# Float64 weight conversion in an attention and two-layer expert kernel: upper words scaled by 2^-112 on ScalarE, clamp pass on VectorE left out

## The chip, the cores and the metric

The kernel runs on one core of one Trainium2 chip. The metric is the device time of one execution in microseconds. Five engines work side by side: TensorE (PE in the rows, its weight loads PEld), VectorE (DVE), ScalarE (ACT), GpSimd (POOL) and the DMA queues, most of which SyncE (SP) issues. Each engine works through its own instructions in the order of the program.

## The reference

The reference is a sliding-window attention (4 batches, 8 heads, 576 positions, head size 64, window 64) and, on its 2304 x 512 output, two gated layers one after the other:

```python
x = attention(q, k, v)                               # 2304 x 512
g = x @ moe_w_gate
x = (g / (1 + exp(-g)) * (x @ moe_w_val)) @ moe_w_out
g = 1 / (1 + exp(-(x @ moe2_w_gate)))
out = (g * (x @ moe2_w_val)) @ moe2_w_out
```

q, k and v are float32. [...]

## The kernel before, in words

Each weight matrix is cut into 12 blocks of 128 x 512 numbers; with six matrices that makes 72 conversions. One conversion goes like this. SyncE loads the block as pairs of words into a tile `raw` (`load_raw`, L374); there are four such tiles, so the load for a later block waits until the conversion four blocks earlier has read its tile for the last time. `round_a` then puts two instructions on ScalarE: L392 reads the lower words as unsigned integers, scales them by 2^-29 and writes integers, which gives the rounded lowest bits; L395 copies the upper words, read as if they were float32, into a tile `t` with the sign taken off (`Abs`). `round_b` puts four on VectorE: L403 picks the sign bit out of a 16-bit quarter of each number and sets the top exponent bit beside it; L404 clamps `t` between 2^-15 and 122816; L405 shifts `t` left by 3 bits; L406 adds the words that L392 and L403 wrote. The result is the weight in float32. L404 reads what L395 wrote, L405 reads what L404 wrote, and L406 reads what L405 wrote.

All products run in a split form: a float32 operand is cut into an upper part that ScalarE copies (`split_hi` L430 for weights, `x_hi` L343 for attention output, L970 for the hidden values) and the rest, which VectorE subtracts (`split_lo` L434, `x_lo` L346, L888). Three products of parts make one product.

The program is written out as a hand-made schedule. It has these stages:

- The start: the attention of the first four blocks of 128 tokens, with the first six conversions between them, in the order of the list `START` (`ca` is `round_a`, `cb` is `round_b`, `hi` and `lo` are L343 and L346, `ch` and `cl` the weight splits).
- The first layer, in five tiles of 512 or 384 tokens. Each tile has 12 rounds of three groups of 12 matmuls on TensorE: gate product (L448), value product (L448), output product (L459). Beside each group a table of due steps (`before`, `during`, `after`, filled by `at`) adds other work to the queues: the attention of the next tile's blocks and conversions. All remaining 30 conversions of the first layer's weights lie in the first of these tiles, which ends near 165 us in the profile; the second layer's 36 lie in the tiles after it, until 531 us.
- The second layer (L781, L846), which works on weights that are already converted.

The attention of one block takes these steps: transposes into PSUM (L205), copies out of it on ScalarE (`qt` L214, `kt` L220), scores (L247), masking on VectorE (L266), exponentials on ScalarE (L284, with an activation table load of its own), normalizing (L305 on ScalarE in the first tile, L309 on VectorE elsewhere), transposes (L317), copies (L323) and the product with v (L333). ScalarE also does the gate function (L961, which has a table load of its own) and stores each split output weight to DRAM (`store_parts`, L417). From the first tile to the end of the second, SyncE also rearranges q and k of later blocks through DRAM in many small pieces (`to_squares`, L136).

Of the kernel before, what the change touches and what calls it, by code (L numbers as in the profile page):

```python
# [8 lines left out]
FP32 = mybir.dt.float32  # L9
# [4 lines left out]
ACTF = mybir.ActivationFunctionType  # L14
ALU = mybir.AluOpType
# [1 line left out]
DRAM = bass.MemoryType.DRAM  # L17


F64_LEAST = 2.0 ** -15  # L20
F64_MOST = 122816.0

# [15 lines left out]
def attention_moe_moe(  # L40
# [20 lines left out]
    nc = tc.nc  # L61
# [7 lines left out]
    scale = 1.0 / float(D) ** 0.5  # L69
# [307 lines left out]
    def words_of(r):  # L377
        w = r.rearrange("p (f two) -> p f two", two=2)
        half = r.bitcast(UINT16).rearrange("p (f four) -> p f four", four=4)
        return w[:, :, 0], w[:, :, 1], half[:, :, 1], half[:, :, 3]  # L380
# [6 lines left out]
    def round_a(key):  # L387
        t = t_p.tile([128, 512], INT32, tag="t", name="t")
        mids[key] = t
        if wide:  # L390
            lower, upper, _, _ = words_of(raws[key])
            nc.scalar.activation(  # L392
                out=lower, in_=lower.bitcast(UINT32), func=ACTF.Copy, scale=2.0 ** -29
            )
            nc.scalar.activation(out=t.bitcast(FP32), in_=upper.bitcast(FP32), func=ACTF.Abs)  # L395

    def round_b(key):
        r = raws.pop(key)
        t = mids[key]
        tf = t.bitcast(FP32)  # L400
        if wide:
            lower, _, second, fourth = words_of(r)
            nc.vector.tensor_scalar(second, fourth, 0x8000, 0x4000, ALU.bitwise_and, ALU.bitwise_or)  # L403
            nc.vector.tensor_scalar(tf, tf, F64_LEAST, F64_MOST, ALU.max, ALU.min)  # L404
            nc.vector.tensor_scalar(t, t, 3, None, ALU.logical_shift_left)  # L405
            nc.vector.tensor_tensor(out=t, in0=t, in1=lower, op=ALU.add)  # L406
        else:
            nc.vector.tensor_copy(tf, r)
        mids[key] = tf
# [150 lines left out]
    def conv_b(j):  # L560
        round_b(convs[j][1])
        raw_ahead(j + 1 + 4)

    for j, (s, key) in enumerate(convs[SPLIT_EARLY:], SPLIT_EARLY):
        at(during, s + 1, round_a, key)
        at(during, s + 2, round_b, key)
        at(during, s + 2, raw_ahead, j + 1 + 4)
        plan_split(s + 2, key)
        if key[1] == "o":
            at(during, s + 5, store_parts, key)  # L570
# [20 lines left out]
    def operands(u, j, nm, following):  # L591
# [34 lines left out]
        def away(k):  # L626
# [3 lines left out]
            nc.sync.dma_start(out=wd[j, k][:, "gv".index(nm)], in_=stages[k][0].bitcast(FP32))  # L630

        at(during, u - 4, round_a, keys[0])
        at(during, u - 3, round_b, keys[0])
        at(during, u - 1, sums, 0)
        at(during, u - 1, upper, 0)
        at(during, u - 1, round_a, keys[1])
        at(during, u, lower, 0)
        at(during, u, round_b, keys[1])
# [253 lines left out]
    with tc.manual_schedule():  # L892
# [4 lines left out]
        t = ps_m.tile([128, 512], FP32, tag="a3", name="warm")  # L897
# [141 lines left out]
```

## Time and profile before

| what | value |
|---|---|
| time, median of 3 runs | 975.62 us |
| lowest and highest run | 974.51 and 978.52 us |
| profiled execution, span from first to last instruction | 977.2 us |
| mean granted TensorE clock in it | 0.985 of full speed |
| busy: TensorE, VectorE, ScalarE | 949.6, 646.1, 464.8 us |

The page gives no other time for the profiled execution than its span, so the span stands for it here. Busy time of TensorE counts a matmul from its start to its modelled end, and matmuls overlap, so a busy share near 100% doesn't say that every slot is used. A line such as L448 is a line of the kernel above; "<-ACT z L305" behind an idle time names the instruction that ended it.

### The profile page before, as it was taken

The numbers are of one execution on the slowest core, as the hardware profiler recorded it, in microseconds if no ns is written. First come the engines' busy times: TensorE is split into PE (matmuls) and PEld (weight loads), VectorE is DVE, ScalarE is ACT, GpSimd is POOL, SyncE is SP. The second block draws the span as 40 slices with busy tenths as digits, with TensorE's granted clock in tenths as the row PEclk, the third lists the DMA queues.
The fourth block names the chain that finished last, engine by engine and source line by source line (L and its number), as shares of the span: only waits on it lengthen the run. The fifth ranks groups of instructions, "written<-read, shape, count | busy, mean of one in ns | idle before, by whom it ended". The sixth has DMA issues, their size and how long they took to land.

```text
span 977.2 us, 15819 instructions
## 1 busy us (share of the span) xinstructions
PE 949.6 (97%) x5693; PEld 846.6 (87%) x5693; DVE 646.1 (66%) x1473; ACT 464.8 (48%) x1042; POOL 19.8 (2%) x39
## 2 busy tenths in 40 slices
PE   8799999999999999999999999999999999999998
PEld 6677777898878887888899999998899988999986
DVE  6999995656765666656566566688366695566742
ACT  6797985765555555356344331245212253222332
POOL 2101010000000000000000000000000000000000
PEclk7899999999999999999999999999999999999999
DMA  9677796999967664874689757634876625867411
GB/s 223 193 217 238 234 261 166 306 248 233 302 222 223 196 206 136 287 241 147 223 288 382 246 184 253 236 114 130 278 267 227 224 81 198 286 236 251 141 33 64
DMA packets 191774, 210.63 MB, mean 216 GB/s; under 512 B 93136, under 2 KB 135632, under 8 KB 191696
## 3 DMA queue, kind: packets, MB, share of 16 engines
q1 hardware_dynamic: 185360, 199.27, 64.5%
q10 hardware_dynamic: 5376, 7.21, 2.0%
q0 software_dynamic: 960, 3.15, 1.1%
q8 instruction: 45, 0.74, 0.3%
q14 instruction: 33, 0.27, 0.1%
HBM read 168.69 MB, written 46.40 MB: 220 GB/s over the span
## 4 chain that ended last, share of the span: by engine, by line
PE 80%; ACT 9%; DVE 6%; DMA 2%; issue 1%; SPq 0%; ACTq 0%; DVEq 0%
PE a L781 13%; PE g L448 12%; PE a L459 11%; PE v L448 11%; PE att L781 7%; PE a L846 7%; PE att L846 3%; PE v L781 3%; PE g L781 3%; ACT z L284 3%; PE g L846 3%; PE v L846 3%; PE att L333 1%; PE att L247 1%; DMA raw<-in_moe_w_out_dram 1%
## 5 line engine op out<-in xcount | busy, mean ns | idle before, releaser
L448 PE MATMUL g<-x,wg 128*128 128x512 f32 (+1 forms) x720 | 161.9, 374 | 0.8 <-ACT x L343 0.7
L448 PE MATMUL v<-x,wv 128*128 128x512 f32 (+1 forms) x720 | 161.9, 373 | 0.0
L459 PE MATMUL a<-h,wo 128*128 128x512 f32 (+1 forms) x720 | 161.2, 372 | 0.0
L448 PEld LDWEIGHTS g<-x,wg 128*128 128x128 f32 x720 | 133.0, 191 | 19.3 <-ACT x L343 0.8
L448 PEld LDWEIGHTS v<-x,wv 128*128 128x128 f32 x720 | 131.1, 190 | 16.8
L459 PEld LDWEIGHTS a<-h,wo 128*128 128x128 f32 x720 | 129.5, 188 | 18.5 <-issue 1.9
L781 PE MATMUL a<-xs,wop 128*128 128x384 f32 x756 | 136.2, 334 | 0.0
L781 PEld LDWEIGHTS a<-xs,wop 128*128 128x128 f32 x756 | 131.5, 188 | 0.1
L968 DVE TENSOR_TENSOR s<-s,v 128x512 f32<-128x512 f32 (+1 forms) x60 | 38.0, 633 | 104.1 <-PE v L448 74.1
L773 ACT ACTIVATE s<-s 128x384 f32<-128x384 f32 x72 | 37.9, 526 | 82.2 <-DVE s L767 82.2
L781 PE MATMUL att<-xs,wop 128*128 128x384 f32 x384 | 71.7, 334 | 0.0
L846 PE MATMUL a<-wo,hs 128*128 128x512 f32 x288 | 71.2, 389 | 0.0
L970 ACT ACTIVATE h<-s 128x512 fp32r<-128x512 f32 (+1 forms) x60 | 35.1, 585 | 75.4 <-DVE s L968 75.4
L961 ACT ACTIVATE s<-g 128x512 f32<-128x512 f32 (+1 forms) x60 | 33.2, 554 | 76.3 <-PE g L448 75.8
L781 PEld LDWEIGHTS att<-xs,wop 128*128 128x128 f32 x384 | 67.1, 188 | 0.1
L846 PEld LDWEIGHTS a<-wo,hs 128*128 128x128 f32 x288 | 54.0, 188 | 11.1
L403 DVE TENSOR_SCALAR raw<-raw 128x512 uint16<-128x512 uint16 x72 | 54.3, 755 | 6.5 <-ACT raw L392 6.3
L284 ACT ACTIVATE z<-z,nm 128x128 f32<-128x128 f32 x144 | 55.8, 390 | 3.2 <-DVE nm L266 3.0
L392 ACT ACTIVATE raw<-raw 128x512 int32<-128x512 uint32 x72 | 48.2, 669 | 9.6 <-DMA raw<-in_moe_w_out_dram 8.9
L406 DVE CUSTOM_DVE_ANT_0 t<-raw,t 128x1024 uint16<-128x1024 uint16 x72 | 50.1, 696 | 2.5
L767 DVE TENSOR_TENSOR s<-s,a 128x384 f32<-128x384 f32 x65 | 35.1, 553 | 22.9 <-PE a L781 22.6
L430 ACT ACTIVATE wo<-tw 128x512 fp32r<-128x512 f32 x36 | 22.6, 627 | 54.1 <-PE a L846 26.0
(131 smaller groups left out, 1323.3 us busy)
## 6 DMA issues: line engine op xcount, KB each, us to landing
wop<-wd SPq DMA_DIRECT2D x126, 512.0 KB, 5.9
wo<-k0o SPq DMA_DIRECT2D x48, 512.0 KB, 5.0
wd<-stage SPq DMA_DIRECT2D x36, 512.0 KB, 5.1
raw<-in_moe_w_gate_dram SPq DMA_DIRECT2D x24, 512.0 KB, 5.4
raw<-in_moe_w_val_dram SPq DMA_DIRECT2D x24, 512.0 KB, 5.5
raw<-in_moe_w_out_dram SPq DMA_DIRECT2D x24, 512.0 KB, 5.0
tw<-k1o SPq DMA_DIRECT2D x36, 256.0 KB, 3.0
k0o<-wo ACTq DMA_DIRECT2D x12, 512.0 KB, 5.1
```

Of the source, the lines that this page charges most:

```text
L284: nc.scalar.activation(out=z[:, hp, :], in_=z[:, hp, :], func=ACTF.Exp, scale=-1.0, bias=nm[:, hp:hp + 1], accum_out=su[:, hp:hp + 1],)
L392: nc.scalar.activation(out=lower, in_=lower.bitcast(UINT32), func=ACTF.Copy, scale=2.0 ** -29)
L403: nc.vector.tensor_scalar(second, fourth, 0x8000, 0x4000, ALU.bitwise_and, ALU.bitwise_or)
L406: nc.vector.tensor_tensor(out=t, in0=t, in1=lower, op=ALU.add)
L448: nc.tensor.matmul(out=ps[:, 0:n], lhsT=w[:, a, c, :], rhs=xt[:, b, c, 0:n], start=(j == 0), stop=(j == len(mm) - 1),)
L459: nc.tensor.matmul(out=acc[e][:, 0:n], lhsT=w[:, a, e * 128:(e + 1) * 128], rhs=h[:, b, 0:n], start=(fc == 0 and j == 0), stop=(fc == FC - ...
L767: nc.vector.tensor_tensor(out=to[out], in0=to[a], in1=ps, op=ALU.add)
L773: nc.scalar.activation(out=to[which], in_=to[which], func=ACTF.Sigmoid)
L781: nc.tensor.matmul(out=ps, lhsT=w[:, val, a, c, :], rhs=xops[op, b][:, c], start=(n == 0), stop=(n == len(mm) - 1),)
L846: nc.tensor.matmul(out=acc[e], lhsT=h[e // 3][:, a, e % 3 * 128:(e % 3 + 1) * 128], rhs=w[:, b], start=(fc == 0 and n == 0), stop=(fc == F ...
L968: nc.vector.tensor_tensor(out=s, in0=s, in1=vps[:, 0:n], op=ALU.mult)
L970: nc.scalar.activation(out=h[:, 0, 0:n], in_=s, func=ACTF.Copy)
```

## The change

The upper words are no longer read with the sign taken off. ScalarE copies them with a scale of 2^-112 (the same kind of instruction with another function and another scale), which brings the exponent to the place where the shift by 3 leaves a valid float32; the sign goes out with the shift. The clamp on VectorE is left out. The sign pass keeps its mask and drops the second operation.

```diff
-F64_LEAST = 2.0 ** -15
-F64_MOST = 122816.0
+F64_BIAS = 2.0 ** -112
...
     def round_a(key):
...
-            nc.scalar.activation(out=t.bitcast(FP32), in_=upper.bitcast(FP32), func=ACTF.Abs)
+            nc.scalar.activation(
+                out=t.bitcast(FP32), in_=upper.bitcast(FP32), func=ACTF.Copy, scale=F64_BIAS
+            )
...
     def round_b(key):
...
-            nc.vector.tensor_scalar(second, fourth, 0x8000, 0x4000, ALU.bitwise_and, ALU.bitwise_or)
-            nc.vector.tensor_scalar(tf, tf, F64_LEAST, F64_MOST, ALU.max, ALU.min)
+            nc.vector.tensor_scalar(second, fourth, 0x8000, None, ALU.bitwise_and)
             nc.vector.tensor_scalar(t, t, 3, None, ALU.logical_shift_left)
             nc.vector.tensor_tensor(out=t, in0=t, in1=lower, op=ALU.add)
```

VectorE loses 72 instructions, one per conversion. Every other instruction keeps its place in the order of its engine. The shift, which waited for the clamp, now waits for ScalarE's copy.

## Rows read from the trace of the kernel before

**Rows 1.** The page, part 1: busy time, share and instructions of each engine.

```profile
PE 949.6 (97%) x5693; PEld 846.6 (87%) x5693; DVE 646.1 (66%) x1473; ACT 464.8 (48%) x1042; POOL 19.8 (2%) x39
```

**Rows 2.** Windows: stretch, length, busy PE, PEld, DVE, ACT, POOL, clock, DMA, GB/s.

```profile
50.00:100.00 50.00, 49.11 (x295) 39.58 (x288) 47.88 (x116) 43.12 (x96) 5.97 (x7) 0.97 0.73 230
100.00:150.00 50.00, 47.58 (x262) 37.61 (x261) 48.84 (x110) 44.51 (x100) 4.87 (x5) 0.97 0.85 243
```

**Rows 3.** Waits of PE, 41 to 165 us: total, times, longest.

```profile
PE att L247 <- ACT kt L220: 3.3, 3, 2.1
PE att L317 <- ACT z L305: 2.1, 2, 1.3
PE att L247 <- DVE x L346: 1.1, 1, 1.1
PE g L448 <- ACT x L343: 0.7, 1, 0.7
PE att L205 <- ACT qt L214: 0.7, 1, 0.7
```

**Rows 4.** Waits of PE, 165 us to the end.

```profile
PE att L333 <- ACT pt L323: 5.7, 3, 2.1
PE att L317 <- DVE z L309: 1.4, 4, 1.0
PE att L247 <- DVE x L346: 1.2, 1, 1.2
```

**Rows 5.** Timeline of DVE, one conversion: start, duration, what.

```profile
81.83 0.76 DVE L403 TENSOR_SCALAR raw<-raw 128x512 uint16<-128x512 uint16 x1
82.37 0.47 DVE L404 TENSOR_SCALAR t<-t 128x512 f32<-128x512 f32 x1
82.87 0.43 DVE L405 TENSOR_SCALAR t<-t 128x512 int32<-128x512 int32 x1
```

**Rows 6.** Groups by line and shape on ACT: busy, mean ns, idle before.

```profile
L392 ACT ACTIVATE raw<-raw 128x512 int32<-128x512 uint32 x72 | 48.2, 669 | 9.6 <-DMA raw<-in_moe_w_out_dram 8.9 <-DMA raw<-in_moe_w_gate_dram 0.8
L395 ACT ACTIVATE t<-raw 128x512 f32<-128x512 f32 x72 | 47.7, 663 | 0.0
```

**Rows 7.** Timelines of ACT and PE at the end of the start.

```profile
40.40 0.60 ACT L343 ACTIVATE x<-a 128x512 fp32r<-128x512 f32 x1
46.77 1.28 ACT L961 ACT_TABLE_LOAD   x1 [2.15 <-DVE wo L434]
...
44.70 2.98 PE L448 MATMUL v<-x,wv 128*128 128x512 f32 x12
49.78 1.59 PE L247 MATMUL att<-kt,qt 64*64 64x128 f32 x32 [2.10 <-ACT kt L220]
```

**Rows 8.** Timeline of ACT, 84 to 104 us.

```profile
84.06 0.63 ACT L430 ACTIVATE wv<-t 128x512 fp32r<-128x512 f32 x1 [1.02 <-DVE t L406]
...
94.41 0.63 ACT L430 ACTIVATE wv<-t 128x512 fp32r<-128x512 f32 x1 [1.45 <-DVE t L406]
...
96.07 0.58 ACT L961 ACTIVATE s<-g 128x512 f32<-128x512 f32 x1
...
103.24 1.26 ACT L305 ACTIVATE z<-z,su 128x128 f32<-128x128 f32 x4
```

**Rows 9.** Timeline of PE around 100 us, and the window of the lower clock.

```profile
94.05 2.88 PE L448 MATMUL v<-x,wv 128*128 128x512 f32 x12
...
104.64 4.59 PE L448 MATMUL v<-x,wv 128*128 128x512 f32 x12
...
104.90:108.30 3.40, 3.40 (x9) 2.61 (x9) 3.30 (x9) 3.40 (x9) 0.00 (x0) 0.50 0.48 107
```

**Rows 10.** SP's waits, 60 to 150 us; the window 155 to 160 us; ACT near 227 us.

```profile
SPq L374 <- DVE t L406: 41.4, 20, 3.5
...
155.00:160.00 5.00, 4.31 (x32) 3.22 (x28) 0.16 (x1) 2.29 (x4) 0.00 (x0) 1.00 0.30 49
...
226.95 0.65 ACT L392 ACTIVATE raw<-raw 128x512 int32<-128x512 uint32 x1 [2.84 <-DMA raw<-in_moe_w_out_dram]
```

## The prediction

> **What bounds the kernel now.** I read the page first. TensorE is busy for 949.6 of 977.2 us, VectorE for 646.1 [rows 1]. Over the whole kernel VectorE has a third of its time to spare, so work taken from it can only help in a stretch where it is late. The windows show that there is one: from 50 to 150 us VectorE is busy for 47.9 and 48.8 of 50 us, and ScalarE for 43.1 and 44.5 [rows 2]. That is the first tile of the first layer, into which all 30 remaining conversions of its weights are packed.
>
> Whether being late costs anything is in the waits of TensorE. From its first gate product at 41 us to the end of that tile at 165 us it stands still for 3.3 + 2.1 + 1.1 + 0.7 + 0.7 = 7.9 us [rows 3], and from there to the end for 5.7 + 1.4 + 1.2 = 8.3 us [rows 4]. So the change cannot be worth the 36 us of clamps that it takes out. It is worth the part of the first sum that a late VectorE causes, what it moves in the start, and what the clock gives back.
>
> **The change, part by part.**
>
> *The clamp.* In one conversion L403 starts at 81.83, L404 at 82.37 and L405 at 82.87 [rows 5]. L405 waits for the result of L404, which is why 0.50 us lie between their starts. Without L404 the shift needs only ScalarE's copy, done well before, so it can start where L404 did: 0.50 us less per conversion, 72 x 0.50 = 36 us on VectorE, 15 us of it in the 30 conversions of the first tile.
>
> *The sign pass.* It touches the same elements with one operation instead of two. No row has that form. Of two passes over one shape, L404 with two operations takes 0.47 us and L405 with one 0.43 [rows 5], on other types; so I take 0, with 0.04 per conversion as the gain at most and, since the row's own scatter is that size, as the loss at most.
>
> *ScalarE's copy.* Copy with a scale on strided words is what L392 already does, in 669 ns; L395 takes 663 ns [rows 6]. I take 0. The bounds are 6 ns more each (0.2 us over 36 conversions) and the same less.
>
> *The start.* Five conversions lie on VectorE between 25 and 44 us, so at most 5 x 0.50 us are won there, 2.8 us with one clamp that took longer. The last of them stands right before the weight splits for which ScalarE's table load at 46.77 waits [rows 7], and behind that load come the gate function and the copy of kt that ends TensorE's wait of 2.10 us at 49.78. That one counts in full: 0.5 us is the lower end. For the four before it, VectorE must wait at each lower half of x for ScalarE's upper half, the last of which is at 40.40 [rows 7]. Following the timeline forward with the clamps out, I find that about 1.0 us is left of them there, as TensorE's products with v and ScalarE's exponentials stand between. I take 1.0 + 0.5 = 1.5 us; the value product, 44.70, moves up by nearly 1 us with it, so a wait of some 1.5 us stays where 2.10 is now. The ends are 0.5 and 2.8.
>
> *The waits of the first tile.* Two waits for kt are left, 3.3 - 2.1 = 1.2 us [rows 3]. They sit behind ScalarE's L430, which itself waited for a conversion (1.02 us at 84.06 [rows 8]). From 72 us on, VectorE works without a gap, and by 84 us four clamps are out: 2.0 us against a wait of 0.8. I take all 1.2 us.
>
> The waits for L305 are 1.3 and 0.8 us, 2.1 together [rows 3]. The first goes like this. ScalarE waits 1.45 us for a conversion at 94.41, reaches the gate function at 96.07, and after that works without a break through the exponentials to L305 at 103.24 [rows 8]. The gate product was finished by about 94.3, since the next one starts at 94.05 [rows 9]. So ScalarE is 1.8 us later than its input, and the wait behind it is 1.3 us. VectorE has 3.5 us less to do by then. The margin is small: TensorE comes 0.8 us earlier too, so L305 must move up by 2.1 us, and its input allows 1.8 + 0.8 = 2.6. I take the 1.3 us as gone. The second wait has the same shape 40 us later; I take its 0.8 us too. The waits for L346 and qt (1.1 + 0.7) come after copies that start the moment TensorE is done; no conversion is ahead of them, so they stay.
>
> *The clock.* Right behind the wait of 1.3 us the granted clock is 0.50, the level of 1.2 GHz, from 104.9 to 108.3, and the value product there takes 4.59 us [rows 9] against 2.98 in the start [rows 7]: 1.6 us lost. If the wait goes, this fall goes.
>
> *Later tiles.* The waits there follow ScalarE's exponentials, late raw tiles (2.84 us at 226.95 [rows 10]) and products, not the clamp. I take 0, with 1 us either way.
>
> *Transfers.* A raw tile is free when its conversion is done, and SyncE waited 41.4 us for that [rows 10], so loads start earlier too and run together with the rest. They share the DMA engines with the small pieces of q and k, busy at 0.85 in the second half [rows 2]. Between 155 and 160 us the share drops to 0.30 [rows 10]: the backlog has drained, so the second tile's transfers start with its work, wherever that lies. I cost this at nothing; that gap is the cover.
>
> **The sum.** 1.5 (start) + 1.2 (kt) + 2.1 (L305) = 4.8 us, and 1.6 for the clock makes 6.4 us, or 977.2 - 6.4 = 970.8 us for the profiled execution. The median of the runs, 975.6 us, is 1.6 us under its span, as much as one fall of the clock costs. Whether the median run had the fall at 105 us cannot be seen. I count half of it: 975.6 - 4.8 - 0.8 = 970.0 us.
>
> **The rivals.** Half a percent, 4.9 us, is about what a measurement of this kernel can tell from no change: faster means under 970.7 us, slower over 980.5.
>
> 1. *TensorE is the bound, and nothing moves.* For it: 97% busy [rows 1]; a wait that goes could come back at the next buffer. Against it: the waits of rows 3 name instructions that stand behind conversions. It gives 975.6 us; chance 0.10. The Trainium skill, "Perfetto Trace Analysis", section "Identifying the Most-Contended Engine", holds that the engine with the highest occupancy is the most contended and is to be optimized first. By that rule the clamp is on the wrong engine and the time stays; the windows of rows 2 differ, since VectorE is as busy there as TensorE.
>
> 2. *ScalarE takes VectorE's place.* It has 5 to 7 us of 50 to spare there [rows 2], and the margin at L305 is half a microsecond. If the waits for L305 stay, and the clock with them, only 1.5 + 1.2 = 2.7 us are won: 972.9 us. Chance 0.27.
>
> 3. *More than I count.* All 2.8 us of the start, and its shorter wait keeps the clock up as well, another 1.6: 975.6 - (2.8 + 1.2 + 2.1 + 1.6 + 1.6) = 966.3 us. Chance 0.13.
>
> 4. *Slower: the transfers do not move up.* If the stream of small pieces holds its pace in time, TensorE runs ahead of it, and the waits at late raw tiles grow by what was won, 4.8 us. Longer waits then bring the lower clock where it now stays up, as it did behind 1.3 us: at four of the waits in rows 3 and 4 (the two for L346, two of the three for pt) 4 x 1.6 = 6.4 us, so 975.6 - 4.8 + 4.8 + 6.4 = 982.0 us. It decides once the DMA share stays near 1 through 160 us instead of falling. The 0.30 speaks against it. Chance 0.05.
>
> That the change doesn't do what it says is hardly open: the instruction is gone, and the new copy has the form of L392, ahead of which no table load stands.
>
> **How the numbers follow.** My own forecast, 970.0 us, has a chance of 0.45 and reaches by itself from 968.4 to 971.7 us: the clock counted in full or not at all, and the start at 0.5 to 2.8. About four in five of it, 0.36, lie under 970.7, near enough that I call this a close matter. Faster: 0.36 + 0.13 and a little of rival 2, 0.50. Slower: 0.05 less what falls under the bound, 0.04. The same: the rest, 0.46. The range leaves out the far half of rival 3, most of rival 1 and rival 4: 967.0 to 975.0 us.
>
> **What would show it.** In the profile after, L405 starts 0.53 us behind L403, and no L404 is there. The wait ahead of the first scores after the start is near 1.5 us instead of 2.10, the two waits for L305 and the two short ones for kt are gone, and the first tile ends some 6 us earlier, near 159 us. Behind it the waits of rows 4 stand as they are, so that the difference at 165 us is the difference at the end. The prediction is wrong if VectorE still works without a gap from 72 to 150 us, if ScalarE's idle time there does not fall, or if the 6 us shrink between 160 and 260 us.

## The result

The changed kernel takes 966.81 us (median of 6 runs, 963.98 to 971.0) against 975.62 us before in the same comparison (974.51 to 978.91): a ratio of 0.9913 with a 95% interval of 0.9891 to 0.9934, or 8.5 us less (6.4 to 10.6). It is faster, to which the prediction gave a chance of 0.50. The forecast was 970.0 us with a range from 967.0; the median lies 0.2 us under that low end, and the ratio times 975.62, 967.1 us, just inside.

The page of the profile after, whose span is 965.8 us, against [rows 1]:

```profile
PE 944.8 (98%) x5693; PEld 843.4 (87%) x5693; DVE 616.1 (64%) x1401; ACT 464.2 (48%) x1042; POOL 21.1 (2%) x39
```

VectorE is busy 30 us less, with 72 instructions fewer. One conversion on its timeline (start, duration), against [rows 5]. The lines have moved by one, so L404 is now the sign pass, L405 the shift and L406 the addition; the last row is the addition of the conversion of [rows 5], before:

```profile
74.74 0.75 DVE L404 TENSOR_SCALAR raw<-raw 128x512 uint16<-128x512 uint16 x1
75.27 0.47 DVE L405 TENSOR_SCALAR t<-t 128x512 int32<-128x512 int32 x1
75.77 0.69 DVE L406 CUSTOM_DVE_ANT_0 t<-raw,t 128x1024 uint16<-128x1024 uint16 x1
...
83.33 0.69 DVE L406 CUSTOM_DVE_ANT_0 t<-raw,t 128x1024 uint16<-128x1024 uint16 x1
```

The shift starts 0.53 us behind the sign pass, where the clamp did. From the sign pass to the addition it is 1.03 us (74.74 to 75.77), where it was 1.50 (81.83 to 83.33): 0.47 us less and not 0.50, since the addition now starts 0.50 us behind the shift, where it was 0.46. The groups by line and shape show what the two other edits cost (mean ns behind the busy time; before, [rows 6], and 755 ns for the sign pass):

```profile
L404 DVE TENSOR_SCALAR raw<-raw 128x512 uint16<-128x512 uint16 x72 | 54.6, 759 | 4.3 <-ACT raw L391 4.0
L394 ACT ACTIVATE t<-raw 128x512 f32<-128x512 f32 x72 | 48.0, 666 | 0.0
```

Next to nothing: 4 and 3 ns more. The first tile's windows, against [rows 2], and the gap in the transfers at its end, against [rows 10] (columns: stretch, length, busy PE, PEld, DVE, ACT, POOL, clock, DMA, GB/s):

```profile
50.00:100.00 50.00, 49.93 (x282) 40.19 (x279) 46.31 (x114) 47.09 (x109) 6.75 (x6) 1.00 0.81 239
100.00:150.00 50.00, 49.25 (x307) 39.67 (x306) 42.05 (x88) 45.05 (x95) 4.56 (x5) 1.00 0.86 241
...
147.00:152.00 5.00, 4.31 (x42) 3.47 (x38) 0.09 (x1) 2.47 (x5) 0.00 (x0) 1.00 0.34 56
```

VectorE has come down from 48.8 to 42.1 of 50 us in the second window. From 72 to 150 us, where it waited for nothing before, it now waits 5.3 us in nine places, and ScalarE's waits for VectorE there are down from 10.9 to 3.4 us. The gap in the transfers came 8 us earlier, with the work. TensorE's waits from 38 to 160 us, and then those behind, against [rows 3, 4]. The first row lies ahead of the 41 us at which [rows 3] begin; before, that wait was 1.3 us:

```profile
PE a L332 <- DVE x L345: 1.9, 1, 1.9
PE att L246 <- DVE x L345: 1.1, 1, 1.1
PE g L448 <- ACT x L342: 0.8, 1, 0.8
PE att L204 <- ACT qt L213: 0.7, 1, 0.7
...
PE att L332 <- ACT pt L322: 3.4, 3, 1.6
PE att L316 <- DVE z L308: 1.4, 4, 1.0
PE att L246 <- DVE x L345: 1.2, 1, 1.2
```

The waits for kt and for L305 (now L304) are gone, those behind copies stand. The timelines of ScalarE, and below it of TensorE, show the chain of [rows 8, 9] again:

```profile
79.94 0.63 ACT L430 ACTIVATE wv<-t 128x512 fp32r<-128x512 f32 x1 [0.56 <-DVE t L406]
...
91.08 0.60 ACT L961 ACTIVATE s<-g 128x512 f32<-128x512 f32 x1 [1.34 <-PE g L448]
...
98.26 1.27 ACT L304 ACTIVATE z<-z,su 128x128 f32<-128x128 f32 x4
...
99.05 0.87 PE L316 MATMUL att<-ident,z 128*128 128x128 f32 x4
99.67 3.00 PE L448 MATMUL v<-x,wv 128*128 128x512 f32 x12
```

ScalarE now waits 1.34 us for the gate product instead of coming 1.8 us late to it; the transposes follow without a wait, and the value product behind them takes 3.00 us, not 4.59.

**Where the time went**, by the starts of products on TensorE's timeline: the first two gate products (the second ends the start), the first one of the second tile, the first one of the third tile, the last one of the first layer. The column "pt" has TensorE's waits for pt, all of them in the second tile. Every profiled execution of this study, in us:

| profile | first gate product at | from it to the second | first tile | second tile | pt | third tile to the last gate product |
|---|---|---|---|---|---|---|
| before | 41.1 | 10.3 | 114.0 | 98.9 | 5.7 | 291.3 |
| before, again (e5) | 39.5 | 9.7 | 113.4 | 96.4 | 4.6 | 291.2 |
| clamp back in all (e1) | 40.9 | 10.4 | 113.9 | 94.2 | 1.6 | 291.2 |
| clamp back in first layer (e3) | 39.1 | 10.3 | 113.6 | 96.7 | 5.0 | 291.2 |
| clamp back in the start (e7) | 40.7 | 10.6 | 108.4 | 95.6 | 3.8 | 291.2 |
| clamp back in second layer (e4) | 40.5 | 9.2 | 107.6 | 94.6 | 3.0 | 291.3 |
| only the clamp out (e2) | 40.8 | 9.2 | 107.6 | 96.5 | 3.2 | 291.3 |
| changed | 40.8 | 9.2 | 107.6 | 95.1 | 3.4 | 291.3 |
| changed, again (e10) | 38.2 | 9.2 | 107.8 | 97.2 | 3.9 | 291.3 |
| changed, raw loads earlier (e6) | 40.4 | 9.2 | 109.3 | 93.0 | 1.6 | 291.2 |
| changed, fewer of them (e9) | 40.1 | 9.2 | 108.0 | 94.1 | 2.2 | 291.3 |
| two passes in first layer (e8) | 41.9 | 11.6 | 125.0 | 95.0 | 3.2 | 291.2 |

The first tile takes 113.4 to 114.0 us with the clamp in it and 107.6 to 108.4 without (109.3 in e6, for a late transfer told of below): 6 us. From the first gate product to the second it is 9.7 to 10.6 us with the clamp in the start and 9.2 without. The time of the first gate product scatters by 2 to 3 us with and without. The second tile scatters by nearly 5 us among the kernels with the raw loads where they were, and not by the clamp: less its waits for pt it takes 91.4 to 91.9 us in the eight profiles in which the granted clock stayed up there, and 92.6 to 93.3 in the four in which it fell once to 0.50 (before, e1, e2, e10).

### The profile page after: what moved, and what is told of

Its sections match the earlier page's. It is cut to its first block, busy times and chain, and to the rows that moved or that the text cites. A ratio compares the mean times of both kernels' runs of the same rounds, so it can differ in the third digit from the quotient of the medians.

```text
span 965.8 us, 15744 instructions
## 1 busy us (share of the span) xinstructions
PE 944.8 (98%) x5693; PEld 843.4 (87%) x5693; DVE 616.1 (64%) x1401; ACT 464.2 (48%) x1042; POOL 21.1 (2%) x39
## 4 chain that ended last, share of the span: by engine, by line
PE 87%; ACT 8%; DVE 2%; DMA 2%; issue 1%; ACTq 0%; DVEq 0%
PE a L781 14%; PE g L448 13%; PE a L459 13%; PE v L448 12%; PE att L781 7%; PE a L846 7%; PE att L846 3%; PE v L781 3%; PE g L781 3%; PE g L846 3%; PE v L846 3%; ACT z L283 2%; PE att L332 2%; PE att L246 1%; DMA raw<-in_moe_w_out_dram 1%; ACT L283 1%
## 5 line engine op out<-in xcount | busy, mean ns | idle before, releaser
L404 DVE TENSOR_SCALAR raw<-raw 128x512 uint16<-128x512 uint16 x72 | 54.6, 759 | 4.3 <-ACT raw L391 4.0
L406 DVE CUSTOM_DVE_ANT_0 t<-raw,t 128x1024 uint16<-128x1024 uint16 x72 | 49.9, 694 | 2.5
```

Of the source, the lines that this page charges most:

```text
L404: nc.vector.tensor_scalar(second, fourth, 0x8000, None, ALU.bitwise_and)
```

## The experiments

**Which of the three edits it is.** e1 puts a clamp pass that changes no value into the changed kernel; e2 takes only the clamp out of the kernel before.

```diff
+            nc.vector.tensor_scalar(tf, tf, -3e38, 3e38, ALU.max, ALU.min)
             nc.vector.tensor_scalar(t, t, 3, None, ALU.logical_shift_left)
```

> The changed kernel with a clamp pass put back on VectorE in all 72 conversions, between bounds that change no value (-3e38 and 3e38); ScalarE's scaled copy and the shorter sign pass stay. If the clamp pass is the whole of it (mine): back to about 975.6 us, within 2 us, the waits of TensorE for kt and L305 in the first tile return. If the scaled copy or the shorter sign pass carries part: well below, at the extreme still 966.8 us.

Measured: 974.25 us, ratio to before 0.9997 (0.9981 to 1.0013). TensorE's waits before 165 us and, in the last line, behind it:

```profile
PE att L246 <- ACT kt L219: 3.3, 3, 2.1
PE att L316 <- ACT z L304: 2.0, 2, 1.3
...
PE att L332 <- ACT pt L322: 1.6, 1, 1.6
```

```diff
-            nc.vector.tensor_scalar(tf, tf, F64_LEAST, F64_MOST, ALU.max, ALU.min)
```

> The kernel before with nothing but the clamp pass taken out; ScalarE still takes the sign off and the sign pass keeps both operations. If the clamp pass is the whole of it (mine): 966.8 us, within 2 us. If the scaled copy or the sign pass carries the gain: 975.6 us.

Measured: 967.4 us, ratio 0.9922 (0.99 to 0.9945). The clamp pass carries the gain. The theory that the scaled copy and the shorter sign pass carry it falls twice; a part of theirs under some 2 us, the half width of these intervals, would not show.

**Which conversions.** e3 puts the neutral pass back in the first layer's conversions, e4 in the second layer's, e7 in the six of the start.

```diff
+            if key[0] == 0:      # e4: key[0] == 1; e7: early[0]
+                nc.vector.tensor_scalar(tf, tf, -3e38, 3e38, ALU.max, ALU.min)
             nc.vector.tensor_scalar(t, t, 3, None, ALU.logical_shift_left)
```

> The changed kernel with the neutral clamp pass put back in the first layer's 36 conversions alone (the start and the first tile). If what is won lies there, and the shorter waits at late raw tiles of the second tile only follow from transfers that moved up (mine): nearly everything is given back, 974 to 976 us. If the second layer's own shorter conversions shorten those waits: they stay short, 2 to 4 us of the gain stay, 971 to 973 us.

Measured: 975.77 us, ratio 1.0019 (1.0003 to 1.0036): everything given back, with the second layer's conversions still without the clamp.

> The changed kernel with the neutral clamp pass put back in the second layer's 36 conversions alone. Mine: no change from the changed kernel, 966 to 968 us, waits for pt of about 3.4 us in all as there. If the second layer's shorter conversions shorten those waits: they return to about 5.7 us, with a fall of the clock, 969 to 971 us.

Measured: 968.86 us, ratio 0.9939 (0.9917 to 0.9961), with waits for pt of 3.0 us in its profile. The median lies between the two branches. Its interval holds the ratio of the changed kernel in e10 (0.9925) and just misses the first one (0.9913), so by the medians a cost of 1.4 to 2.5 us can't be excluded. The profile shows none: start, first and second tile are as in the changed kernel. And e3, which has no clamp in these conversions, gains nothing by it.

> The changed kernel with the neutral clamp pass put back in the first six conversions alone, which lie in the start. By my term for the start, 1.5 us, or 2.3 as the difference after the third gate product says: 968.3 to 969.1 us, and a wait for kt near 2.1 us back ahead of the first scores. If a late start is made up in the first tile: 966.8.

Measured: 969.21 us, ratio 0.9943 (0.9923 to 0.9964); the wait of 2.1 us for kt is back. Against the changed kernel's two ratios, 0.9913 and 0.9925, that is 1.8 to 2.9 us, but the intervals overlap. The profiles say it more closely: from the first gate product to the second tile e7 takes 118.9 us, the changed kernel 116.8 and 117.0. So the six conversions of the start are worth 2.0 to 2.1 us, 0.6 to 0.7 of them behind the start, in the first tile. Behind the wait for kt the clock fell. TensorE's scores and gate product in e7, and in the changed kernel:

```profile
49.43 1.90 PE L246 MATMUL att<-kt,qt 64*64 64x128 f32 x32 [2.09 <-ACT kt L219]
51.25 3.83 PE L450 MATMUL g<-x,wg 128*128 128x512 f32 x12
...
48.98 1.10 PE L246 MATMUL att<-kt,qt 64*64 64x128 f32 x32
50.01 3.06 PE L448 MATMUL g<-x,wg 128*128 128x512 f32 x12
```

The granted clock is 0.50, the level of 1.2 GHz, from 49.6 to 53.0 us in e7, and scores and product take 1.6 us more. The scores themselves start 8.75 us behind the first gate product in e7 and 8.14 in the changed kernel: 0.6 us. Together these are the 2 us, and the delay is not made up later.

**How near VectorE is to being the bound.** e8 puts two neutral passes into the first layer's conversions.

> The changed kernel with two neutral clamp passes, not one, in the first layer's 36 conversions. If VectorE is the bound there from 50 to 150 us (its busy share before was 48 to 49 of 50): the second pass is paid nearly in full, 30 x 0.5 in the tile and 2 to 3 in the start, so 12 to 18 us above the kernel before, 987 to 993 us. If TensorE is the bound and VectorE only a little late at some places: about as much as the first pass cost, 7 us, so 982 us.

Measured: 988.35 us, ratio 1.0143 (1.0113 to 1.0173), 13.5 us over the kernel before. Its windows and TensorE's waits before 165 us:

```profile
50.00:100.00 50.00, 45.12 (x270) 36.16 (x271) 47.07 (x105) 39.61 (x83) 6.83 (x7) 0.93 0.65 193
100.00:150.00 50.00, 42.82 (x226) 33.96 (x226) 48.65 (x115) 37.73 (x79) 4.26 (x5) 0.90 0.80 234
...
PE att L246 <- ACT kt L219: 9.7, 3, 3.6
PE att L316 <- ACT z L304: 3.3, 1, 3.3
```

The first pass in the tile's 30 conversions costs 6 us, the second 11 (125.0 against 113.7, the mean with one pass). In these windows VectorE's busy time does not rise over [rows 2], TensorE's falls. The whole first tile in the changed kernel, in the kernel before and in e8 (columns as above):

```profile
50.01:157.64 107.63, 105.73 (x640) 84.80 (x637) 92.61 (x222) 93.53 (x204) 12.19 (x12) 1.00 0.82 236
51.30:165.28 113.98, 108.90 (x640) 86.73 (x638) 104.48 (x250) 93.33 (x204) 10.49 (x12) 0.97 0.76 224
53.50:178.53 125.03, 112.78 (x641) 89.52 (x637) 116.36 (x280) 94.07 (x203) 10.12 (x12) 0.94 0.71 202
```

Each pass adds 11.9 us to VectorE's busy time. The second lengthens the tile by 11.0 us, nearly as much; the first by 6.3 us. For without the pass TensorE stands still for only 1.9 of 107.6 us and is itself the bound. So the kernel before stood at the knee: part of each clamp was still hidden by TensorE, and that cover was nearly used up. TensorE's clock is lower in e8, 0.94 on average against 0.97, and its busy time 3.9 us longer; how much of the 11.0 us that makes is not separated.

**What the second tile's scatter is.** e5 is the kernel before, profiled once more.

> The kernel before, looked at once more, for what differs between two looks at one kernel. If the waits at late raw tiles (TensorE waits for pt behind 165 us) belong to the kernel: 5.7 us again. If they hang on how the transfers fall in an execution (mine, from the kernel with the clamp pass put back, where they were 1.6): anywhere from 1.6 to 6 us. The waits before 165 us are the same in both cases, 3.3 for kt and 2.1 for L305.

Measured, in one execution: 973.75 us, and among TensorE's waits behind 165 us

```profile
PE att L333 <- ACT pt L323: 4.6, 3, 1.9
```

With the clamp in the second layer's conversions these waits were 5.7, 4.6, 1.6 (e1) and 3.0 us (e4), without it 3.4, 3.9 (e10), 3.2 (e2), 5.0 (e3), 3.8 (e7) and 3.2 (e8): with a mean of 3.7 and 3.8 us they do not follow the clamp, and one kernel has 5.7 and 4.6. That they hang on how the transfers fall in an execution fits this; it is not shown by itself.

e6 and e9 move the raw loads that they wait for.

```diff
-        at(during, g - 5, load_raw, key)
+        at(during, g - 7, load_raw, key)      # e9: g - (7 if fc >= 3 else 5)
```

> The changed kernel with the raw loads of the second layer's output weights issued two steps earlier (7 instead of 5 steps ahead). If the late raw tiles of the second tile come from a load queue that is behind (mine): the waits for pt behind 165 us fall to the one of 1.6 us in every look, and the median falls by 1 to 2 us, to 965 to 966. If the loads are late because the DMA engines are full there: they stay at 3 us or more, and the time at 966.8.

Measured: 965.11 us, ratio 0.9908 (0.9889 to 0.9928). The waits for pt are down to the one of 1.6 us, and the second tile is the shortest of the study, 93.0 us. The first tile lost 1.7 us in this profile, though, to another late raw tile, which ScalarE waits for at 129 us, and a wait for L304 behind it:

```profile
129.08 0.70 ACT L391 ACTIVATE raw<-raw 128x512 int32<-128x512 uint32 x1 [2.49 <-DMA raw<-in_moe_w_gate_dram]
```

> The changed kernel with the raw loads of the second layer's output weights issued two steps earlier from the fourth block on; the first three stay where they are. Two steps earlier for all of them took the late waits for pt away (1.6 us left, by copies alone) and brought a wait for L305 of 1.1 us back at the end of the first tile, where its loads mix with those of the first layer. If that wait comes from the first three loads: it is gone here, the waits for pt stay at 1.6, and the median is 963 to 965 us, 2 to 3 under the changed kernel on the same chip. If it was chance: no better than the kernel with all loads earlier, 965 to 966.

> The changed kernel once more, beside the one with later loads moved and the kernel before, on one chip. 966 to 968 us; waits of TensorE ahead of 165 us as in its first look (1.1 and 0.7 behind copies, none for kt or L305 above 1.5), waits for pt behind it anywhere from 1.6 to 4 us.

Measured side by side: e9 965.69 us, ratio 0.9905 (0.9888 to 0.9922); e10 967.22 us, ratio 0.9925 (0.99 to 0.9949). In e9 the wait for L304 is gone, but the waits for pt are 2.2 us, not 1.6, and the median is that of the other branch: of three points the first held. With earlier loads the late waits are short in both profiles, 1.6 and 2.2 us; e1, with the loads where they were, has 1.6 too, so two profiles do not prove the loads to be the cause. The ratios of both versions are 0.0005 to 0.0020 below the changed kernel's, 0.5 to 2.0 us, and their intervals overlap. Whether the first tile pays for the first three loads is not settled by one profile each.

## Why the prediction was right, and what it sized wrong

*Which stretch, and why.* Right. VectorE's total of 36 us counted for little, the 100 us in which it was as busy as TensorE for nearly all of it: from the third tile on, every profile has 291.2 or 291.3 us, with or without the clamp. Rival 1, TensorE as the bound, falls. The Trainium skill's rule of the most-contended engine ("Perfetto Trace Analysis", "Identifying the Most-Contended Engine"), taken over the whole kernel, pointed the other way; the same page's section "Optimization Strategy" says that the most-contended engine can change over time, and the 6 us of the tile bear that out.

*The clamp's cost per conversion.* 0.50 us of spacing forecast, 0.47 measured, with 30 us less busy time and a shift that starts where the clamp did: right but for the shift, which takes 470 ns on average where it took 439. *Sign pass and copy at nothing.* Right, by 4 and 3 ns and by e2.

*The start, 1.5 us.* The number is near the 2.0 to 2.1 us that e7 and the table give, by luck, for they are other microseconds. The half microsecond of the last conversion is right: the scores start 8.7 us behind the first gate product in every profile with one clamp pass there and 8.1 in every one without. The 1.0 us from the four conversions before it is not shown: the first gate product stands at 39.1 to 41.1 us with them and at 38.2 to 40.8 without. What the sum put at nothing, without a reason, is the clock behind the wait of 2.10 us. In the kernel before it is 0.50 from 50.3 to 53.7 us, the scores take 1.59 us [rows 7] and the gate product behind them

```profile
51.30 4.10 PE L448 MATMUL g<-x,wg 128*128 128x512 f32 x12
```

instead of 1.10 and 3.06: 1.5 us. This fall is there in four of the five profiles with one pass in the start (not in e5), and in none of the six without. Only rival 3 had counted it. The wait left in the changed kernel depends on the clock ahead of it. In the first profile of the changed kernel the first gate product fell into a stretch at 1.2 GHz and took 4.48 us, and no wait was left ahead of the scores (next two rows); in e10 it ran at full clock, and the wait stands at 1.5 us as the prediction said (the rows behind):

```profile
40.84 4.48 PE L448 MATMUL g<-x,wg 128*128 128x512 f32 x12 [0.76 <-ACT x L342]
...
48.98 1.10 PE L246 MATMUL att<-kt,qt 64*64 64x128 f32 x32
```

```profile
41.89 2.99 PE L448 MATMUL v<-x,wv 128*128 128x512 f32 x12
46.39 1.10 PE L246 MATMUL att<-kt,qt 64*64 64x128 f32 x32 [1.51 <-ACT kt L219]
```

*The waits for kt and L305.* Both went, as did the fall of the clock behind the first one: right, and rival 2 (ScalarE takes VectorE's place) falls, though ScalarE is at 47.1 of 50 us. But the sum of 1.2 + 2.1 us for waits and 1.6, counted half, for the clock makes 4.1, where the tile gave 6.3 in these two profiles. The waits were right: by the tile's windows under e8 TensorE stands still for 5.1 us before and 1.9 after, 3.2 less. But it was also busy for 3.2 us less, and of that the sum had only 0.8. This is the term that was mis-sized, and three things lay in it: the fall at 105 us in full, 1.6 us; the end of the fall behind the start's wait, 1.0 us (4.10 against 3.06 above); and the transposes behind the two waits for L305, about 0.6 us. The second of these waits on TensorE, before and then after:

```profile
140.62 2.88 PE L448 MATMUL g<-x,wg 128*128 128x512 f32 x12
144.28 1.21 PE L317 MATMUL att<-ident,z 128*128 128x128 f32 x4 [0.77 <-ACT z L305]
...
148.08 0.60 PE L317 MATMUL att<-ident,z 128*128 128x128 f32 x4
...
151.29 2.88 PE L448 MATMUL g<-x,wg 128*128 128x512 f32 x12
```

```profile
134.22 2.89 PE L448 MATMUL g<-x,wg 128*128 128x512 f32 x12
136.95 0.93 PE L316 MATMUL att<-ident,z 128*128 128x128 f32 x4
...
143.66 2.88 PE L448 MATMUL g<-x,wg 128*128 128x512 f32 x12
```

The transposes behind the wait stand 1.21 us in the rows as busy, and the four of the next group 0.60: those behind the wait start 0.29 us apart, as ScalarE's four instructions on their parts do. So from one gate product to the next the changed kernel is 1.2 us shorter, 9.44 against 10.67, and not 0.8.

Nor are wait and clock terms that simply add. In e3 the clock did not fall in the second window, and its tile took 113.6 us all the same, with longer waits for kt, 4.3 us in all:

```profile
100.00:150.00 50.00, 46.88 (x264) 36.88 (x263) 48.56 (x110) 44.98 (x97) 3.85 (x5) 1.00 0.85 235
...
PE att L246 <- ACT kt L219: 4.3, 3, 2.1
```

With a fall TensorE works slower, without one it waits longer; with the clamp in, VectorE's pace sets the tile. The tile's length was the quantity to forecast, not the sum of TensorE's waits in one profile.

*Later tiles and transfers, 0 with 1 us either way.* The two profiled executions differ there by 3.8 us (98.9 against 95.1), which was outside that, and so the 7.6 us between them at the end of the first tile are 11.4 at the end of the kernel. By the table it is scatter: 2.3 us of waits for pt and one fall of the clock at 255 us, and e1 has the clamp and the shortest second tile of the kernels with the loads where they were. The transfers moved up with the work, and rival 4 did not happen.

*The sum.* Its own ends add up to 967.9 and 971.8 us, not to 968.4 and 971.7: 1.3 us more or 1.0 less from the start, and 0.8 either way from the clock. The remark that the median lies 1.6 us under the span, as much as one fall of the clock costs, sets two different times side by side: every run here whose span is listed took 1.7 to 1.9 us more than its span, so the profiled execution took about 979.0 us and the median was 3.4 us shorter. It is no ground for counting the clock half.

*The measured size.* From the first gate product to the second tile the profiles with the clamp take 123.1 to 124.3 us, the changed kernel 116.8 and 117.0: 6.1 to 7.5 us. By e7 2.0 to 2.1 of them are the start's conversions, the rest the tile's. Most of that lies in the interval of 6.4 to 10.6; whether the rest up to the median of 8.5 us is won ahead of the first gate product or is scatter can't be told. Rival 3 (9.3 us) lies in it too. It was right that the clock would stay up at both places, and is not borne out on the 2.8 us of the start.

## What to carry to other kernels

Ask for each stretch which engine is full, not for the whole kernel; an engine at 66% overall was worth 8 us here because one stretch of 100 us used 96 to 98% of it. Where two engines are nearly full in a stretch, the waits of the bound engine in one profile are not the whole of what the other one costs it: half of the 6.3 us stood in the rows as busy time, at the lower clock and in instructions that wait piece by piece. A doubled pass shows how near the second engine is to being the bound: removing a pass that kept VectorE busy for 11.9 us gave 6 us, and adding one cost 11. Before explaining a difference between two profiles, profile the same kernel twice; here the start and one tile changed by 2 to 3 us from one execution to the next.

## What the runs showed of the hardware

Executions of one kernel on one core differ by more than I had expected, and the granted clock differs with them. Of the nine runs of e10 the fastest took 964.5 us at a mean clock of 0.998, the slowest 974.7 at 0.988. The stretches at 1.2 GHz lie at different places in two profiles of one kernel: behind the first 40 us, the changed kernel has one at 40.6 us in the first profile and one at 242 us in the second, each for 3.4 us. In the kernel before, a wait of 1.3 us was followed by such a stretch [rows 9], and so were the one of 2.10 us ahead of the scores and one of 2.09 us at 254 us, while one of 2.00 us at 229 us was not; products of 384 columns took 3.88 us behind the one and 2.35 behind the other:

```profile
229.10 1.15 PE L333 MATMUL att<-pt,v 128*64 128x64 f32 x30 [2.00 <-ACT pt L323]
230.18 2.35 PE L448 MATMUL g<-x,wg 128*128 128x384 f32 x12
...
254.02 1.15 PE L333 MATMUL att<-pt,v 128*64 128x64 f32 x30 [2.09 <-ACT pt L323]
255.09 3.88 PE L448 MATMUL g<-x,wg 128*128 128x384 f32 x12
```

From one profile it can't be said which wait will cost clock.
